# Chunk attention with a two-layer MLP: a list scheduler in the source, and both layers of the MLP by seven products

## The chip, the cores and the metric

One core of one Trainium2 chip. The time is device time in microseconds (us) of one launch. Three runs of the kernel before took 285.93, 286.01 and 288.08 us; their median, 286.01, is the time before. Lines written L171 are lines of the kernel before, unless the kernel after is named.

## The reference

```python
scores = scale * np.matmul(q_c, k_c.transpose(0, 1, 2, 4, 3))
scores = scores - np.max(scores, axis=-1, keepdims=True)
attn = np.exp(scores)
attn = attn / (np.sum(attn, axis=-1, keepdims=True) + 1e-09)
out = np.matmul(attn, v_c)
...
x = np.ascontiguousarray(attn_out.transpose(0, 2, 1, 3)).reshape(B * S, H * D)
...
h = x @ w_in
g = np.maximum(0.01 * h, h)
return (g @ w_out).astype(np.float32)
```

q, k and v are 8 batches x 8 heads x 576 tokens x 64; each chunk of 64 tokens attends only to itself, with scale 1/8. The result, put side by side over the heads, is x of 4608 tokens x 512. Then comes an MLP: w_in is 512 x 2048, w_out 2048 x 512, with a leaky ReLU between, here called the first and the second layer. The output is 4608 x 512 in fp32.

## The kernel before, in words

*Attention* goes by groups of 128 tokens (two chunks, all 8 heads): 36 groups, numbered u = 0 to 35. POOL issues the loads of q, k (L73) and v (L82), and of both weights (L89, L101), cast to fp16 on the way; only the first group's q and k come as fp32 through other queues. TensorE (PE) needs q and k turned. For the first nine groups (UD = 9) PE turns them (L542, L547) and VectorE (DVE) and ScalarE (ACT) copy them out; for the rest SP issues DMA transposes (stage_t, L567), and POOL copies q into the zero-padded tile QZ (L576). Then, for each group: scores on PE (L583); on DVE their maximum mx (L593) and its subtraction sh (L598); the exponential ex on ACT (L605); on DVE the row sum z (L612), the small constant ze (L614), the reciprocal zi (L616) and the normalization en (L622). en is turned by PE for the first nine groups (L631, with the copy et at L638), by a DMA transpose that SP issues for the others (L644). The values product xp = et x v follows on PE (L657), and ACT copies it into the ring xT of 1536 tokens (L673), the input of the first layer.

*The MLP* goes by blocks of tokens: six of 128, three of 256, six of 512 (BLOCKS). The first layer is always the plain product (mm1, L171): four 128-row steps for each 128 of the 2048 hidden units, 512 columns of PSUM to a unit of work; ACT applies the leaky ReLU while it copies PSUM to gT in fp16 (act1, L191). The second layer of the blocks of 128 and 256 is the plain product (mm2, L203). For the six blocks of 512 tokens it goes by seven products instead of eight (Strassen's way, L298): g is cut into 2 x 2 parts (256 tokens x 1024 hidden units), w_out into 2 x 2 parts (1024 x 256), and each product multiplies a part, or a sum of parts, of each. The sums of w_out (WF, L234) are made once. DVE makes the sums of gT for each block (form, L263), 128 x 2048 elements each. The products go into three PSUM tags, ma, mb and mc, two banks of work at a time; DVE and ACT combine them (combine, L334 to L343; evict, L352 to L356) into the output tile osb. The last block does this in halves (piece, L364 to L390), so that its stores go out in pieces.

*The order* is written in two ways. For the first groups it stands by hand in a string (FRONT, L724), with idle products between (L681). From group 5 on a loop over groups (L757 to L787) fixes where each group's attention stages go, and fill(n) puts units of MLP work on PE between them. pick() takes the first unit whose inputs are due by running sums of the time that PE, DVE and ACT have been given (T). Each of eight PSUM banks has a fixed purpose: a tag each for transposed q and k (shared with ma and mb), scores, values, and four for MLP units, of which mc takes one.

## Time and profile before

| | |
|---|---|
| Runs | 285.93, 286.01, 288.08 us |
| Span of the profiled execution | 285.7 us |
| Instructions | 7255 |
| Matmuls and transposes on PE | 3012 |
| Instructions on DVE, ACT, POOL (as counted in the profile) | 322, 264, 166 |
| Moved by DMA | 39.14 MB |

The profiled execution's span lies 0.3 us under the median of the runs. A page gives each engine's busy time, its share of the span and the number of its instructions; groups of instructions by source line, with busy time and the mean duration of one in ns; and the chain of waits, followed back from the last instruction. PEld is the weight load of PE, which runs beside its matmuls. A busy engine is not always one that works at its pace: matmuls are pipelined, and their durations in the trace overlap. Rows such as "52.70 0.89 PE hT L171 x16" of the chain are start, length, engine, tile, line and number of instructions.

### The profile page before, as it was taken

The numbers are of one execution on the slowest core, as the hardware profiler recorded it, in microseconds if no ns is written. First come the engines' busy times: TensorE is split into PE (matmuls) and PEld (weight loads), VectorE is DVE, ScalarE is ACT, GpSimd is POOL, SyncE is SP. The second block draws the span as 40 slices with busy tenths as digits, with TensorE's granted clock in tenths as the row PEclk, the third lists the DMA queues.
The fourth block names the chain that finished last, engine by engine and source line by source line (L and its number), as shares of the span: only waits on it lengthen the run. The fifth ranks groups of instructions, "written<-read, shape, count | busy, mean of one in ns | idle before, by whom it ended". The sixth has DMA issues, their size and how long they took to land.

```text
span 285.7 us, 7255 instructions
## 1 busy us (share of the span) xinstructions
PE 275.5 (96%) x3012; PEld 226.3 (79%) x3012; DVE 193.8 (68%) x322; ACT 149.4 (52%) x264; POOL 128.1 (45%) x166
## 2 busy tenths in 40 slices
PE   4979999999999999999999999999999999999995
PEld 4969855877949585899989899998999998666784
DVE  6987515666687776557888888888888840820392
ACT  6347733655738374777356546554565554535320
POOL 8846646876585647657538495332410000000000
PEclk9999999999999999999999999999999999999999
DMA  9999999999999999999999999999714301200213
GB/s 131 170 189 179 192 165 195 143 180 162 175 147 173 158 156 184 162 157 134 155 154 158 139 188 197 153 136 249 114 30 112 93 2 73 76 0 0 110 59 129
DMA packets 165825, 39.14 MB, mean 137 GB/s; under 512 B 156832, under 2 KB 161440, under 8 KB 165792
## 3 DMA queue, kind: packets, MB, share of 16 engines
q0 software_dynamic: 114336, 18.09, 91.5%
q1 hardware_dynamic: 50416, 20.33, 42.8%
q8 instruction: 23, 0.38, 0.5%
q10 hardware_dynamic: 1040, 0.26, 0.4%
q14 instruction: 10, 0.08, 0.1%
HBM read 36.70 MB, written 9.44 MB: 161 GB/s over the span
## 4 chain that ended last, share of the span: by engine, by line
PE 84%; DMA 6%; DVE 5%; ACT 2%; issue 1%; POOL 1%; ACTq 0%; POOLq 0%
PE hT L171 40%; PE oP L203 15%; PE mb L298 10%; PE mc L298 7%; PE ma L298 6%; DMA k_in<-in_k_dram 4%; PE xp L657 3%; PE Sp L583 2%; DMA VB<-in_v_dram 2%; DVE S L263 2%; ACT ex L605 1%; ACT gT L191 1%; DVE en L622 1%; PE kp L547 1%; DVE sh L598 0%
## 5 line engine op out<-in xcount | busy, mean ns | idle before, releaser
L171 PE MATMUL hT<-xT,w_inT 128*128 128x256 f16 (+2 forms) x1344 | 143.4, 257 | 1.9 <-DMA w_inT<-in_moe_w_in_dram 0.9
L171 PEld LDWEIGHTS <-w_inT 128*128 128x128 f16 x1344 | 107.6, 98 | 15.6 <-issue 2.6
L191 ACT ACTIVATE gT<-hT 128x512 f16<-128x512 f32 x144 | 85.5, 595 | 54.5 <-PE hT L171 53.3
L576 POOL COPY QZ<-QT 64x512 f16<-64x512 f16 x54 | 36.5, 676 | 53.0 <-DMA QT<-q_in 34.1
L203 PE MATMUL oP<-w_outT,gT 128*128 128x512 f16 x192 | 44.9, 379 | 0.0
L298 PEld LDWEIGHTS <-gT 128*128 128x128 f16 x384 | 37.5, 98 | 6.2
L605 ACT ACTIVATE ex<-sh 128x512 f16<-128x512 f32 x36 | 22.6, 627 | 33.7 <-DVE sh L598 33.6
L73 POOL DMA_DIRECT2D k_in<-in_k_dram x39 | 32.9, 845 | 15.9 <-DVE z L612 4.1
L612 DVE TENSOR_REDUCE z<-ex 128x8 f32<-128x512 f16 x36 | 24.7, 685 | 21.1 <-ACT ex L605 20.9
L593 DVE TENSOR_REDUCE mx<-Sp 128x8 f32<-128x512 f32 x36 | 24.7, 686 | 18.1 <-PE Sp L583 18.0
L73 POOL DMA_DIRECT2D q_in<-in_q_dram x39 | 33.2, 851 | 7.0 <-DMA w_outT<-in_moe_w_out_dram 2.4
L298 PEld LDWEIGHTS <-S 128*128 128x128 f16 x288 | 28.1, 98 | 5.0 <-DVE S L263 0.5
L203 PEld LDWEIGHTS <-gT 128*128 128x128 f16 x192 | 17.6, 98 | 17.7
L622 DVE TENSOR_TENSOR en<-ex,zi 128x512 f16<-128x512 f16 x36 | 27.2, 757 | 1.2
L673 ACT ACTIVATE xT<-xp 128x512 f16<-128x512 f32 x36 | 21.3, 592 | 9.4 <-PE xp L657 9.4
L598 DVE TENSOR_TENSOR sh<-Sp,mx 128x512 f32<-128x512 f32 x36 | 24.9, 691 | 1.2
L298 PE MATMUL mb<-WF,gT 128*128 128x256 f16 x192 | 24.6, 273 | 0.0
L263 DVE TENSOR_TENSOR S<-gT 128x2048 f16<-128x2048 f16 x18 | 22.3, 1278 | 1.5 <-ACT gT L191 1.5
L82 POOL DMA_DIRECT2D VB<-in_v_dram x16 | 18.5, 1161 | 0.0
L215 ACT ACTIVATE osb<-oP 128x512 f32<-128x512 f32 x12 | 7.2, 597 | 18.4 <-PE oP L203 18.4
L657 PEld LDWEIGHTS <-VB 128*128 128x128 f16 x288 | 13.1, 98 | 3.1 <-issue 0.6
L583 PEld LDWEIGHTS <-QZ 128*128 128x128 f16 x288 | 13.2, 99 | 2.2 <-issue 0.3
(57 smaller groups left out, 233.2 us busy)
## 6 DMA issues: line engine op xcount, KB each, us to landing
out_dram<-osb SPq DMA_DIRECT2D x10, 512.0 KB, 3.5
VB<-in_v_dram POOLq DMA_DIRECT2D x16, 288.0 KB, 13.2
q_in<-in_q_dram POOLq DMA_DIRECT2D x31, 128.0 KB, 13.1
k_in<-in_k_dram POOLq DMA_DIRECT2D x31, 128.0 KB, 13.6
out_dram<-osb SPq DMA_DIRECT2D x14, 256.0 KB, 6.8
w_inT<-in_moe_w_in_dram POOLq DMA_DIRECT2D x8, 256.0 KB, 9.7
w_outT<-in_moe_w_out_dram POOLq DMA_DIRECT2D x4, 512.0 KB, 9.9
q_in<-in_q_dram POOLq DMA_DIRECT2D x8, 64.0 KB, 9.1
```

The source lines that it names most:

```text
L73: nc.gpsimd.dma_start(out=t[a - r0:z - r0], in_=src[a // S, :, a % S:a % S + z - a, :].rearrange("h p d -> p h d"),)
L171: nc.tensor.matmul(out=hT[:, i, :], lhsT=w_inT[:, t, fc * 128:(fc + 1) * 128], rhs=xT[:, t, r0 % RING:r0 % RING + tb], start=(t == 0), sto ...
L191: nc.scalar.activation(out=gT[j][:, nf * a:nf * a + nf, h * tb:h * tb + tb], in_=HT.pop((j, a, h)), func=AFT.Prelu, bias=0.0, scale=1.0, a ...
L203: nc.tensor.matmul(out=o, lhsT=gT[j][:, fc, ti * 128:(ti + 1) * 128], rhs=w_outT[:, fc, :], start=(n == 0 and fc == part * 4), stop=(n == ...
L263: nc.vector.tensor_tensor(out=to, in0=of, in1=by, op=op)
L298: nc.tensor.matmul(out=BANK[bank][:, p, :] if j < LAST else ENDS[bank, p], lhsT=lhs[:, fc, p * 128:(p + 1) * 128], rhs=rhs[:, fc, :], star ...
L576: nc.gpsimd.tensor_copy(out=QZ[u % NQZ][part, :, :, s, :], in_=qt[part])
L593: nc.vector.tensor_reduce(out=MX[u], in_=SP[u], axis=AXL.X, op=ALU.max)
L598: nc.vector.tensor_tensor(out=SH[u], in0=SP.pop(u), in1=MX.pop(u).unsqueeze(2).to_broadcast((128, 8, CH)), op=ALU.subtract)
L605: nc.scalar.activation(out=E[u], in_=SH.pop(u), func=AFT.Exp, bias=0.0, scale=SCL)
L612: nc.vector.tensor_reduce(out=z, in_=E[u], axis=AXL.X, op=ALU.add)
L622: nc.vector.tensor_tensor(out=E[u], in0=ex, in1=ZI.pop(u).unsqueeze(2).to_broadcast((128, 8, CH)), op=ALU.mult)
```

## The change

The kernel is rewritten. What it computes is the same; these parts differ.

*The order is planned by a program in the source.* Every instruction, or short run of them, becomes a task with an engine (or several that may take it, each with a cost), a key (when it is wanted), the tasks on which it depends and the buffers that it takes. Buffers are rings with as many places as RINGS says; eight PSUM banks form one ring that all uses share. Plan.run walks through time: on each engine it takes, of the tasks that can start first, the one with the lowest key. A task that several engines may take goes to the one where it ends first with what is queued there; so q's copies into QZ, the copies of PSUM, ze and en may go to DVE, ACT or POOL. The keys come from the places of the MLP's units on PE and from a table of numbers, NUDGE.

*The blocks* are four of 128 tokens (0 to 3) and eight of 512 (4 to 11). PE turns the first eight groups instead of nine. q and k have 7 places instead of 9.

*The first layer* of blocks 5 to 11 goes by seven products instead of eight, that of block 4 by the plain product in pieces of 256 tokens, that of blocks 0 to 3 plain. x is cut into 2 x 2 parts (256 of the 512 inputs x 256 tokens), w_in into 2 x 2 parts (256 x 1024). DVE makes four sums of x for each block (xs) and, once, four of w_in (FI). Each block has four chains; in each, three PSUM banks X, Y and V hold two 128-row pieces of hidden units. P5 opens V and is copied to p5; P1 opens X, and X is copied to Y, PSUM to PSUM; P6 is added in X; DVE sets V = X + p5; P7 is added in X; DVE sets w = X + p5; P4 is added in X; P2 is added in Y and P3 in V. Four leaky evictions (c11 from Y, c12 from V, c22 from w, c21 from X) write gT.

*The second layer* of blocks 4 to 11 goes by seven products in another form, whose products also are added in three PSUM banks X, Y and V, in the order P1, P2, P6, P5, P7, P4, P3. It has three sums of w_out (FO), and a fourth that overwrites a part of w_outT. DVE makes the sums S1 to S4 of gT, each in two instructions of 128 x 1024 elements. X is copied to p1, u2 and u3 between its products, and DVE adds them to Y or V into osb. The last block goes in two chains of one 128-token piece each.

The core of the diff:

```diff
+        def behind(t, e, at):
+
+            return self.lean.get(e, 0.0) + max(now[e], at) + t.engs[e] + sum(x.engs[e] for x in ready[e] if x.key < t.key and x.eng == e)
...
+                    ahead = min(loads, key=lambda c: c[1].key)
+                    can = [c for c in can if c not in loads or c is ahead]
+                first = min(c[0] for c in can)
+                c = min((c for c in can if c[0] <= first + slack), key=lambda c: c[1].key)
+                if best is None or c[0] < best[0]:
...
+KNOBS = {'LEAD': 9.24,
+ 'PACE': 3.62,
+ 'UD': 8,
+ 'L1_PLAIN': (0,),
+ 'LEAN': {'DVE': -0.13, 'POOL': -0.48, 'ACT': -0.13},
+ 'LOADS': 'Q0 g3 g7 v0 g1 Q1 g4 Q3 P1 Q2 P0 g6 P2 P3 v1 g5 g2',
+ 'NUDGE': {'s': -3.18,
+           'Q4': -14.46,
+           'zv.0.0': 51.85,
...
+    PLAIN = 4
+    NB = (NU - PLAIN) // 4
...
-    BLOCKS = [128] * 6 + [256] * 3 + [512] * 6
-    PLAIN = 9
...
+    LEAD, PACE, LEAN, NUDGE, LOADS = (KNOBS[n] for n in ("LEAD", "PACE", "LEAN", "NUDGE", "LOADS"))
+    UD, L1_PLAIN = KNOBS["UD"], KNOBS["L1_PLAIN"]
...
+    RINGS = {
+        "bank": 8, "qk": 7, "QT": 4, "KT": 5, "QZ": 3, "mx": 2, "sh": 2, "ex": 2, "z": 2, "en": 4, "et": 4,
+        "xs": 2, "p5": 2, "w": 2, "gT": 2, "S1": 1, "S2": 1, "p1": 1, "u2": 1, "u3": 1, "osb": 3,
+    }
...
+    def need(u):
+        j = block_of(u)
+        back = 0 if j < PLAIN else 3 - (u - PLAIN) % 4
+        return at1[j] - back * PACE - LEAD + NUDGE.get(f"need{u}", 0.0)
...
+
+        ts = task(f"s.{u}", PE, 0.24, key + 0.5, emit_s, deps=ready, bufs=[qz, kt], opens=[sp], bank="full")
+        tm = task(f"m.{u}", DVE, 0.6, key + 0.6, emit_m, deps=[ts], bufs=[sp], opens=[mx])
+        tb = task(f"b.{u}", DVE, 0.6, key + 0.61, emit_b, deps=[tm], bufs=[sp, mx], opens=[sh])
+        tx = task(f"x.{u}", ACT, 0.52, key + 0.7, emit_x, deps=[tb], bufs=[sh], opens=[ex])
+        tz = task(f"z.{u}", DVE, 0.71, key + 0.8, emit_z, deps=[tx], bufs=[ex], opens=[z])
+        tz = task(f"ze.{u}", {DVE: 0.2, POOL: 0.3}, 0, key + 0.801, emit_ze, deps=[tz], bufs=[z])
+        tz = task(f"zi.{u}", DVE, 0.24, key + 0.802, emit_zi, deps=[tz], bufs=[z])
+        tn = task(f"n.{u}", {DVE: 0.61, POOL: 1.0}, 0, key + 0.81, emit_n, deps=[tz], bufs=[ex, z], opens=[en])
...
+            td = task(f"d.{u}", SP, 1.3, key - 15.0, emit_d, deps=[tn], bufs=[en], opens=[et], after=("turn", 0.0, 1))
...
+    fi = sums("fi", DVE, 1.14, (
+        (lambda: FI[:, 0], ADD, lambda: A21, lambda: A22, ()),
+        (lambda: FI[:, 1], SUB, lambda: FI[:, 0], lambda: A11, (0,)),
+        (lambda: FI[:, 2], SUB, lambda: A11, lambda: A21, ()),
+        (lambda: FI[:, 3], SUB, lambda: A12, lambda: FI[:, 1], (1,)),
+    ), [key_fi + i for i in range(4)], [t for x in wi.values() for t in x])
...
+    def forms_out(plain):
+        return sums("fo", DVE, 1.14, (
+            (lambda: FO[:, 0], SUB, lambda: B12, lambda: B11, ()),
+            (lambda: FO[:, 1], SUB, lambda: B22, lambda: FO[:, 0], (0,)),
+            (lambda: FO[:, 2], SUB, lambda: B21, lambda: FO[:, 1], (1,)),
+            (lambda: B12, SUB, lambda: B22, lambda: B12, (0,)),
+        ), [key_fo + i for i in range(4)], [t for x in wo.values() for t in x] + rows[0] + cv, tail=plain)
...
+        ts = sums("xs", DVE, 0.34, (
+            (lambda: mem(xs)[:, 0], SUB, lambda: x12, lambda: x11, ()),
+            (lambda: mem(xs)[:, 1], SUB, lambda: x22, lambda: mem(xs)[:, 0], (0,)),
+            (lambda: mem(xs)[:, 2], SUB, lambda: x22, lambda: x12, ()),
+            (lambda: mem(xs)[:, 3], SUB, lambda: x21, lambda: mem(xs)[:, 1], (1,)),
+        ), [k0 - 2, k0 - 1, k0, k0 + 1], us, opens=[xs], of=f".{j}")
...
+            P5 = product("P5", "V", FI[:, 0], 0, XS(0), True, 0, [fi[0], ts[0]], [xs], bufs=bufs)
+            P1 = product("P1", "X", w_inT[:, 0:2], 0, lambda: x11, True, 1, us + W, bufs=bufs)
...
+            c5 = task(f"p5.{j}.{n}", MOVE, 0, key + 1.0 * UNIT, move(lambda p5=p5: mem(p5), lambda ps=ps: ps["V"]), deps=[P5], bufs=[bV], opens=[p5])
+            cy = task(f"y.{j}.{n}", MOVE, 0, key + 1.1 * UNIT, move(to_y, lambda ps=ps: ps["X"]), deps=[P1], bufs=[bX], opens=[bY], bank="seed")
+            P6 = product("P6", "X", FI[:, 1], 0, XS(1), False, 2, [cy, fi[1], ts[1]], [xs], bufs=bufs)
+            P2 = product("P2", "Y", w_inT[:, 2:4], 0, lambda: x21, False, 3, [cy] + us + W, bufs=bufs)
+
+            def emit_z(ps=ps, p5=p5):
+                nc.vector.tensor_tensor(out=ps["V"], in0=ps["X"], in1=mem(p5), op=ADD)
+
+            def emit_w(ps=ps, p5=p5, w=w):
+                nc.vector.tensor_tensor(out=mem(w), in0=ps["X"], in1=mem(p5), op=ADD)
+
+            tz = task(f"z.{j}.{n}", DVE, 0.6, key + 2.5 * UNIT, emit_z, deps=[P6, c5], bufs=[bX, bV, p5])
+            P7 = product("P7", "X", FI[:, 2], 0, XS(2), False, 4, [tz, fi[2], ts[2]], [xs], bufs=bufs)
+            P3 = product("P3", "V", FI[:, 3], 0, lambda: x22, False, 5, [tz, fi[3]] + us, bufs=bufs)
+            tw = task(f"w.{j}.{n}", DVE, 0.6, key + 4.5 * UNIT, emit_w, deps=[P7, tz], bufs=[bX, p5], opens=[w])
+            P4 = product("P4", "X", w_inT[:, 2:4], HF, XS(3), False, 6, [tw, ts[3]], [xs], bufs=bufs)
+            readers[j] += [P1, P2, P3]
...
+            evict("Y", 0, 0, 4, [P2], [bY], "c11")
+            evict("V", 0, 1, 6, [P3], [bV], "c12")
+            evict("w", HB, 1, 6.5, [tw], [w], "c22")
+            evict("X", HB, 0, 7, [P4], [bX], "c21")
...
+            ORDER = ("P1", "P2", "P6", "P5", "P7", "P4", "P3")
+            into = {"P1": "X", "P6": "X", "P7": "X", "P4": "X", "P2": "Y", "P5": "V", "P3": "V"}
+            bufs = {"X": bX, "Y": bY, "V": bV}
+            key = {m: k0 + span * i / 7 + shift for i, m in enumerate(ORDER)}
...
-    ORDER = (3, 2, 1, 5, 4, 6, 7)
...
+    for j in range(NJ):
+        if j == PLAIN:
...
+        if j < PLAIN:
+            done = layer1_plain(j, 128)
+            plain += layer2_plain(j, done)
+        else:
+            done = layer1_plain(j, 256) if j - PLAIN in L1_PLAIN else layer1_seven(j)
+            layer2_seven(j, done)
...
-    ROUND = [0] * 6 + [6] * 33
-    for it in range(6, NU + 3):
...
-        if it <= NU:
...
-        due = free_v[:]
-        values(it - 2 if it - 2 < UD else it - 3 if it - 3 >= UD else -1)
-        fill(ROUND[it] - 4)
-        for b in due:
...
+    for emit in plan.run(filler=(filler, emit_idle)):
+        emit()
```

At the start, POOL issues the loads in another order. The kernel before, from v's first batch on (q_in and k_in are a group's rows, VB v's, w_inT x4 two quarters of w_in):

```order
L82 DMA VB_63<-in_v_dram 64x36x64 x2
L73 DMA q_in<-in_q_dram 128x8x64
L73 DMA k_in<-in_k_dram 128x8x64
L89 DMA w_inT<-in_moe_w_in_dram 64x4x512 x4
L73 DMA q_in<-in_q_dram 128x8x64
L73 DMA k_in<-in_k_dram 128x8x64
L89 DMA w_inT<-in_moe_w_in_dram 64x4x512 x4
L73 DMA q_in<-in_q_dram 64x8x64 x2
```

The kernel after, from v's first batch on, behind the first quarter of w_in and groups 3 and 7 (qk is q or k of one group):

```order
L396 DMA VB_114<-in_v_dram 64x36x64 x2
L390 DMA qk_66<-in_q_dram 128x8x64
L390 DMA qk_66<-in_k_dram 128x8x64
L402 DMA w_inT<-in_moe_w_in_dram 64x4x512 x2
L390 DMA qk_67<-in_q_dram 64x8x64 x2
L390 DMA qk_67<-in_k_dram 64x8x64 x2
L402 DMA w_inT<-in_moe_w_in_dram 64x4x512 x2
L408 DMA w_outT<-in_moe_w_out_dram 128x4x512
```

w_in comes in quarters between the groups' loads instead of in two halves, the first quarter ahead of everything, and w_out (w_outT) in single quarters between them.

In the second half of the program, DVE before (two attention groups and, between, the combination of the second layer's products and one sum of gT):

```order
L616 RECIPROCAL zi<-ze 128x8
L622 TENSOR_TENSOR en<-ex,zi 128x512
L336 TENSOR_TENSOR tw<-mc,td 128x512
L263 TENSOR_TENSOR gT<-gT 128x8x256
L593 TENSOR_REDUCE mx<-Sp 128x8
L598 TENSOR_TENSOR sh<-Sp,mx 128x512
L612 TENSOR_REDUCE z<-ex 128x8
L614 TENSOR_SCALAR ze<-z 128x8
L616 RECIPROCAL zi<-ze 128x8
L622 TENSOR_TENSOR en<-ex,zi 128x512
L338 TENSOR_TENSOR tt<-tw,osb 128x512
```

DVE after, in the stage of blocks 5 to 11 (S is a sum for the second layer; bank at L836 is V = X + p5, w at L839 is X + p5, p the copied P5, u and osb the second layer's):

```order
L1003 TENSOR_TENSOR S_107<-gT_104,S_107 128x1024 x2
L836 TENSOR_TENSOR bank<-bank,p_100 128x512
L647 RECIPROCAL z_89<-z_89 128x8
L641 TENSOR_REDUCE z_88<-ex_86 128x8
L836 TENSOR_TENSOR bank<-bank,p_101 128x512
L979 TENSOR_TENSOR osb_111<-bank,p_108 128x2x256
L839 TENSOR_TENSOR w_102<-bank,p_100 128x512
L647 RECIPROCAL z_88<-z_88 128x8
L839 TENSOR_TENSOR w_103<-bank,p_101 128x512
L479 COPY p_100<-bank 128x512
L631 TENSOR_REDUCE mx_82<-bank 128x8
L634 TENSOR_TENSOR sh_84<-bank,mx_82 128x512
```

The additions and copies of the first layer's chains stand between the steps of the softmax, which are now further apart; two of its steps, ze and en, are not on DVE there.

They are on POOL. POOL before, in the same stage, copies q into QZ and issues loads:

```order
L576 COPY QZ_67<-QT 64x8x64 x2
L82 DMA VB_63<-in_v_dram 64x36x64 x2
L73 DMA q_in<-in_q_dram 128x8x64
L73 DMA k_in<-in_k_dram 128x8x64
L576 COPY QZ_65<-QT 64x8x64 x2
L73 DMA q_in<-in_q_dram 128x8x64
L73 DMA k_in<-in_k_dram 128x8x64
```

POOL after (L644 is ze, L650 is en, L390 the loads):

```order
L479 COPY QZ_81<-QT_73 64x8x64
L479 COPY QZ_80<-QT_71 64x8x64 x2
L644 TENSOR_SCALAR z_89<-z_89 128x8
L390 DMA qk_69<-in_q_dram 128x8x64
L650 TENSOR_TENSOR en_90<-ex_87,z_89 128x512
L644 TENSOR_SCALAR z_88<-z_88 128x8
L390 DMA qk_69<-in_k_dram 128x8x64
L650 TENSOR_TENSOR en_91<-ex_86,z_88 128x512
```

ze and en of 25 and 20 of the 36 groups stand in POOL's queue, among the copies and the issuing of loads. In all, DVE has 412 rows' instructions instead of 322, ACT 338 instead of 265, POOL 183 instead of 166.

1381 lines of the change are left out of this document (769 added, 612 removed), and 6 rows, old and new, of the table FRONT.

## The prediction

> **What bounds the kernel now.** I read the page's busy lines first, then busy time by stretches, then the chain of waits, then the groups by shape.
>
> ```profile
> span 285.7 us, 7255 instructions
> PE 275.5 (96%) x3012; PEld 226.3 (79%) x3012; DVE 193.8 (68%) x322; ACT 149.4 (52%) x264; POOL 128.1 (45%) x166
> PEclk9999999999999999999999999999999999999999
> ```
> ```profile
> 0.00:24.00 24.00, 18.14 (x284) 16.70 (x284) 18.68 (x38) 11.86 (x19) 16.83 (x27) 1.00 1.56 167
> 24.00:130.00 106.00, 105.15 (x1202) 79.32 (x1199) 66.97 (x120) 61.34 (x108) 69.33 (x86) 1.00 1.87 168
> 130.00:234.00 104.00, 103.82 (x1152) 93.54 (x1151) 88.11 (x138) 57.81 (x106) 41.90 (x54) 1.00 1.37 136
> 234.00:270.00 36.00, 36.00 (x276) 26.15 (x274) 10.60 (x12) 15.55 (x27) 0.00 (x0) 1.00 0.12 45
> ```
> The columns are stretch, length, then PE, PEld, DVE, ACT, POOL busy, granted clock, DMA share and GB/s. From 24 us on PE is idle for little more than 1 us in 246; VectorE is next, 88.11 of 104 us. TensorE is the bound, at full clock, so the change is priced by PE time taken out, less what PE must newly wait for. A busy PE need not run at its pace, so I take the pace from the chain of waits, where pieces follow without a gap:
>
> ```profile
> 49.65 0.23 PE xp L657 x8
> 51.84 0.86 PE oP L203 x4
> 52.70 0.89 PE hT L171 x16
> 53.60 0.22 PE tpe L631 x4
> 147.86 0.87 PE mb L298 x8
> 280.79 1.76 PE mb L298 x16
> ```
> That is 0.029 us for 64 columns, 0.0556 for 128, 0.109 for 256, 0.216 for 512. The counts:
>
> ```profile
> L171 PE MATMUL hT<-xT,w_inT 128*128 128x256 f16 x768 | 95.8, 273 | 0.2 <-ACT xT L673 0.2
> L203 PE MATMUL oP<-w_outT,gT 128*128 128x512 f16 x192 | 44.9, 379 | 0.0
> L171 PE MATMUL hT<-xT,w_inT 128*128 128x128 f16 x512 | 31.7, 219 | 1.8 <-DMA w_inT<-in_moe_w_in_dram 0.9 <-issue 0.7
> L298 PE MATMUL mb<-WF,gT 128*128 128x256 f16 x192 | 24.6, 273 | 0.0
> L171 PE MATMUL hT<-xT,w_inT 128*128 128x512 f16 x64 | 16.3, 379 | 0.0
> ```
> First layer: 768 x 0.109 + 512 x 0.0556 + 64 x 0.216 = 126.0 us. Second: 192 x 0.216 = 41.5, and six blocks by products, 6 x 7 x 2 x 8 = 672 x 0.109 = 73.2. Together 240.7. Attention adds 36 x 0.46 for scores and values and 27 x 0.22 for transposes: 22.5. So 263.2 of the 285.7 us is necessary PE work; the last product ends at 282.5, a tail of 3.2, and 19.3 is lost, nearly all before 37 us.
>
> **The change, part by part.** *Products.* After, the first layer has 4 x 64 = 256 matmuls of 128 columns, one plain block of 128 of 256, and seven blocks x 28 products x 4 = 784 of 256: 256 x 0.0556 + 912 x 0.109 = 113.6. The second has 64 x 0.216 and 8 x 112 = 896 x 0.109: 111.5. Together 225.1, so 15.6 us go. Eight instead of nine groups turned by PE saves 12 transposes, 0.7. With loss and tail as they are: 285.7 - 16.3 = **269.4**.
>
> *Start.* The first big block needs groups 4 to 7. With both weights, v of two batches and the first group in fp32 that is 4.2 + 7 x 0.26 + 1.15 + 0.77 = 7.9 MB as written. The rate of 0 to 24 us above gives 4.0 MB, and the rest comes at the rate of this row:
>
> ```profile
> 24.00:50.00 26.00, 25.20 (x314) 18.76 (x311) 12.48 (x27) 13.46 (x25) 16.26 (x20) 1.00 1.83 181
> ```
> So 24 + 3.9 / 0.181 = 46 us, with some 28 us of four plain blocks to do until then: 18 us lost, as now. The next eight groups are wanted about 5 us each sooner, with their transposes issued by SP. Bounds 0 (loads run ahead, as now) and 5 (nothing covers it); I take 1.0, near the lower end since the loss computed equals today's.
>
> *Values.* Each group's scores pass DVE, ACT, DVE, POOL or DVE, and a DMA transpose. Before, PE has 15 us of other work in between (first two rows, group 12); after, the order puts 10.9 to 12.0 us of matmuls there for four of the last-needed groups (10.9 for two), over 13.4 elsewhere.
>
> ```profile
> 87.49 0.40 PE L583 MATMUL Sp<-KT,QZ 128*128 128x64 f16 x8
> 102.65 0.40 PE L657 MATMUL xp<-et,VB 128*128 128x64 f16 x8
> ```
> ```profile
> 176.03 0.68 DVE L593 TENSOR_REDUCE mx<-Sp 128x8 f32<-128x512 f32 x1
> 176.75 0.69 DVE L598 TENSOR_TENSOR sh<-Sp,mx 128x512 f32<-128x512 f32 x1
> 178.19 0.69 DVE L612 TENSOR_REDUCE z<-ex 128x8 f32<-128x512 f16 x1 [0.76 <-ACT ex L605]
> 179.36 0.69 DVE L622 TENSOR_TENSOR en<-ex,zi 128x512 f16<-128x512 f16 x1
> 179.97 0.68 DVE L338 TENSOR_TENSOR tt<-tw,osb 128x512 f32<-128x512 f32 x1
> ```
> ```profile
> et<-en SPq DMA_TRANSPOSE x6, 7.5
> ...
> et<-en SPq DMA_TRANSPOSE x4, 2.4
> ```
> From mx to the end of en is 4.0 us; the transpose lands in 7.5 us while loads run (140 to 170 us) and 2.4 when they have stopped (after 210). So 11.5 to 12, plus queueing behind other DVE work, about 1.5. Against the four covers that is 2.7 + 2.7 + 2.0 + 1.6 = 9 us late at most, nothing at 2.4. I take 2.5: loads end about then, and DVE and ACT catch up while PE waits. POOL takes 20 of the 36 normalizations (en), which no row shows on POOL: at least its copy of half the elements, at most twice the DVE row's slowest instance:
>
> ```profile
> 154.75 1.28 POOL L576 COPY QZ<-QT 64x512 f16<-64x512 f16 x2 [0.86 <-PE xp L657]
> 161.48 2.16 POOL L576 COPY QZ<-QT 64x512 f16<-64x512 f16 x2 [3.73 <-DMA QT<-q_in]
> 161.63 1.53 DVE L263 TENSOR_TENSOR S<-gT 128x2048 f16<-128x2048 f16 x1
> 174.90 1.22 DVE L263 TENSOR_TENSOR gT<-gT 128x2048 f16<-128x2048 f16 x1
> ```
> 0.6 to 1.8 us; I take 1.1, inside the 1.5 above. [...]
>
> *Round trips.* Each group of a first layer by products goes P1, copy to a second bank, P6, add, P7, add, P4 (numbers of the code): three trips from PE through ACT or DVE and back, 84 in all. In the order mostly three foreign products stand in each gap, 3 x 0.436 = 1.31 us. A trip needs one such operation, 0.60 on ACT (L191: 595 ns) or 0.68 on DVE, and under 0.1 of hand-over: 0.7 if the engine is free, 1.3 behind one other. DVE decides how often it is free. Between the first sums of blocks 5 and 11 PE has 168 x 0.436 + 75 x 0.872 + 44 x 0.23 = 148.8 us of work. DVE has 240 instructions there: 151 of the 512-element kind above, which follow each other at 0.61 us (179.97 less 179.36), 42 of 1024 fp16 elements at 0.60 (half of 1.13, the start to start of the gT row, up to 1.13), 24 of 512 at 0.33 and 23 short ones at 0.2: 130 us, and some 7 for results that the next one needs: 92%. In the stage from 130 us it is 85% by durations, and (88.1 - 138 x 0.09) / 104 = 73% counted so, since neighbours overlap by 0.09. It is not the bound, but seldom free. Bounds for the trips: 0, and 84 x 0.25 = 21 us. I take 2.5, near the lower end, since 92% still leaves 11 us to catch up.
>
> The row of 161.63 lasts 0.3 longer than that of 174.90, and POOL's copies beside it 0.9 longer in all. [...]
>
> *Rest.* ScalarE has 338 instructions instead of 265 in the order, 73 x 0.6 = 44 us on its 149, 70% of the time. The two folded weight sets cost DVE 8 x 1.2 us (five before) while PE has plain blocks. Stores are as many bytes. The tail ends with a 256 KB store instead of 128 KB: 0 to 1.8 us more, I take 0.6. Sum: 269.4 + 1.0 + 2.5 + 2.5 + 0.6 = **276.0**; the runs' median stands 0.3 above the profiled span, within this.
>
> **Rivals.** *Full cover:* order and buffers hide all trips and values: 269.4 to 271.5. For it: PE idles 1 us in 246 today. Against it: three trips where there was none, and short covers. *Late values:* the 9 us come whole: 269.4 + 1 + 9 + 2.5 + 0.6 = 282.5. For it: 7.5 us of landing until 190 us; against it, only four covers are short. *VectorE bounds:* its waits for ACT's exponentials stay as they are,
>
> ```profile
> ACT ex L605 <- DVE sh L598: 33.6, 21, 2.7
> DVE z L612 <- ACT ex L605: 20.9, 29, 1.5
> ```
> which is 0.6 us a group (20.9 / 36), 13 for 22 groups. [...] For it: 92%; against it, the order puts other DVE work into those gaps. *Slower:* the engine in a round trip is behind two operations instead of one half the time, so that a trip takes 0.25 to 0.3 longer than its cover: 84 x 0.27 = 23, giving 269.4 + 23 + 1.6 = 294. It decides from 0.23 us a trip on (19.5 / 84). For it: engines are in order and DVE is 92% full. Against it: P2, P3 and second-layer products can absorb part.
>
> **How the numbers follow.** My forecast, 271.5 to 281, has 0.60; full cover 0.12; late values 0.08; VectorE as the bound 0.07; slower 0.13. I predict 276.0. The range 269 to 285 takes in both middle rivals and leaves out the slow one. One per cent, about what a measurement here can tell, is 283.1 and 288.9. Faster has 0.60 + 0.12 + 0.07 (half of the middle ones, which straddle 283.1) = 0.79, same 0.08, slower 0.13.
>
> **What would show it.** Right: 912 and 896 matmuls of 256 columns at 0.87 for eight; PE idle by 4 to 8 us after 40 us, in pieces under 1 us before FI and w_inT products (waiting for DVE or ACT) and 1 to 3 us before a values product of blocks 9 to 11 (waiting for DMA et); DVE near 240 to 250 us busy. Wrong: PE idle over 2 us in each block waiting for DVE, en on POOL over 2 us with DVE's reciprocal waiting for POOL, or a first second-layer product later than 42 us.

## The result, and the profile after

The changed kernel takes 306.4 us (median of four runs, 304.7 to 306.8) against 285.97 before: a ratio of 1.069, interval 1.0645 to 1.0735. The forecast of 276.0 us is 30 us off, on the wrong side, and outside its range. Where single runs of an experiment lay over 1.5% above its fastest (one run of the control with half loads took 1021.6 us, unexplained), the times below are medians of the others. The profiled execution took 304.71 us with a span of 302.9, so 17.2 us more span than before.

The busy lines of the page for the kernel after:

```profile
span 302.9 us, 7399 instructions
PE 267.9 (88%) x2925; PEld 232.5 (77%) x2925; DVE 228.5 (75%) x412; ACT 184.9 (61%) x335; POOL 139.7 (46%) x183
PEclk9799999999778899995999999999999999999999
```

PE is busy for less time than before (275.5), but in a longer span, and four stretches ran at half clock (0.50 granted): 11.5 to 15, 80 to 87, 97 to 100 and 138 to 145 us. Where the time went stands in the stages. Kernel before, then after; columns as in the prediction: stretch, length, PE, PEld, DVE, ACT, POOL busy, granted clock, DMA share and GB/s:

```profile
0.00:60.00 60.00, 53.30 (x728) 43.14 (x729) 37.53 (x75) 30.88 (x52) 41.37 (x55) 1.00 1.78 169
60.00:180.00 120.00, 119.82 (x1316) 97.84 (x1314) 91.35 (x151) 70.96 (x126) 76.22 (x97) 1.00 1.85 164
180.00:280.00 100.00, 99.80 (x951) 83.27 (x950) 63.30 (x95) 47.60 (x87) 10.47 (x14) 1.00 0.55 85
```
```profile
0.00:60.00 60.00, 49.05 (x648) 40.96 (x649) 45.77 (x86) 30.88 (x55) 40.05 (x54) 0.97 1.82 177
60.00:180.00 120.00, 100.92 (x1067) 86.28 (x1063) 86.21 (x154) 78.30 (x142) 74.03 (x92) 0.93 1.83 154
180.00:280.00 100.00, 98.98 (x1052) 88.94 (x1050) 85.05 (x151) 69.91 (x128) 25.66 (x37) 1.00 0.58 86
```

Busy time hides slow and filling products, so I count each stage's matmuls in the trace, without those on the tile idle, at the paces of the prediction (0.029 us for 64 columns, 0.0556, 0.109 and 0.216 for 128, 256 and 512). What the stage is longer than that is lost:

| stage, us | work before | lost before | work after | lost after |
|---|---|---|---|---|
| 0 to 60 | 42.4 | 17.6 | 36.9 | 23.1 |
| 60 to 180 | 119.4 | 0.6 | 93.6 | 26.4 |
| 180 to 280 | 99.4 | 0.6 | 98.3 | 1.7 |
| 280 to the span's end | 2.3 | 3.4 | 18.3 | 4.6 |
| sum | 263.5 | 22.2 | 247.1 | 55.8 |

The work fell by 16.4 us, as forecast, and the loss rose by 33.6: 5.5 before 60 us, 25.8 in the middle stage, 2.3 after. That is the 17.2 of the span. Of the 25.8, 18.9 are idle time more than before. Of the other 6.9, an estimated 5.6 are work at half clock: in the three such stretches of this stage PE worked for some 11 us behind its waits. From 180 us on, with the same chains of products, PE loses 1.7 us in 100.

What PE waits for, kernel after (engine and line waited for: us in total, times, longest):

```profile
PE bank L685 <- DMA et<-en: 10.9, 3, 5.4
PE bank L557 <- ACT qk L477: 7.5, 2, 5.4
PE bank L625 <- POOL QZ L479: 7.1, 2, 6.1
```

L685 is the values product of an attention group, L625 its scores, and L557 the transposes of the first group at the start (5.4 us of that wait is the time before the first data, which the kernel before has too: its first transpose runs at 5.12). The longest of the scores' waits and of the values' waits, from PE's timeline:

```profile
83.54 0.61 PE L625 MATMUL bank<-KT,QZ 128*128 128x64 f16 x8 [6.07 <-POOL QZ L479]
...
97.33 0.61 PE L685 MATMUL bank<-et,VB 128*128 128x64 f16 x8 [5.40 <-DMA et<-en]
```

By the order the first is group 12's scores, which wait for the copy of its q by POOL, the second group 11's values. Follow them back on the queues that feed them. POOL:

```profile
69.80 0.88 POOL L390 DMA_DIRECT2D qk<-in_k_dram  x1 [1.00 <-DMA qk<-in_k_dram]
70.67 0.86 POOL L479 COPY QZ<-QT 64x512 f16<-64x512 f16 x1
71.62 0.23 POOL L644 TENSOR_SCALAR z<-z 128x8 f32<-128x8 f32 x1
75.21 0.94 POOL L390 DMA_DIRECT2D qk<-in_q_dram  x1 [3.36 <-DMA VB<-in_v_dram]
78.42 0.88 POOL L390 DMA_DIRECT2D qk<-in_k_dram  x1 [2.26 <-DMA VB<-in_v_dram]
79.31 1.06 POOL L650 TENSOR_TENSOR en<-ex,z 128x512 f16<-128x512 f16 x1
80.67 0.94 POOL L390 DMA_DIRECT2D qk<-in_q_dram  x1 [0.30 <-DMA qk<-in_q_dram]
81.60 0.88 POOL L390 DMA_DIRECT2D qk<-in_k_dram  x1
82.53 0.95 POOL L479 COPY QZ<-QT 64x512 f16<-64x512 f16 x1
```

The copy that releases group 12 is the last row; its input, the transposed q, had landed at 74.83. It stands behind four loads of groups 16 and 19, of which the two of group 16 were issued only when older loads had landed (3.36 and 2.26 us). Group 8's normalization (79.31) stands behind the same two, though its reciprocal had been ready since 72.1, and that is how group 11 came late: its exponential on ACT waited 6.02 us for group 8's normalization, since the tile ex has only two places.

```profile
80.40 0.63 ACT L638 ACTIVATE ex<-sh 128x512 f16<-128x512 f32 x1 [6.02 <-POOL en L650]
```
Group 11's own normalization follows on POOL at 85.25. SP, in the same stretch:

```profile
73.32 0.56 SPq L888 DMA_DIRECT2D out_dram<-osb  x1
80.43 1.19 SPq L578 DMA_TRANSPOSE QT<-qk  x1
81.73 1.21 SPq L578 DMA_TRANSPOSE KT<-qk  x1
83.03 1.33 SPq L675 DMA_TRANSPOSE et<-en  x1
84.46 1.28 SPq L578 DMA_TRANSPOSE KT<-qk  x1
85.85 1.46 SPq L578 DMA_TRANSPOSE QT<-qk  x1
87.40 3.90 SPq L675 DMA_TRANSPOSE et<-en  x2
```

SP issues nothing for 6.5 us: the transpose of group 15's q waits for its load, which landed at 80.38. The transpose of group 14's k stands behind it, though its load had landed at 69.24. The transposes of the normalized scores of groups 8, 10 and 11 stand there too, but these scores were ready only at 80.4, 83.0 and 86.3. Group 11's is the second of 87.40; issued by 91.3, landing some 6 us later. Both queues hold back ready work because a load in front of it is late. How late is shown by the time from issue to landing of four loads issued from 41 to 46 us and of four issued from 63 to 66, the last of them group 17's k. The first line answers for the early ones, the second for the late ones (both by tile; the second takes in three DMA transposes too, and its four loads alone took 17.0 to 17.4 us):

```profile
DMA to landing us min/median/max: 7.7/7.9/8.3
```
```profile
DMA to landing us min/median/max: 7.2/17.0/17.4
```

By issue and landing times about eight loads are under way in both stretches, and the landing takes twice as long. Two halves of v are ahead of the late four, which by the fit given with the experiments are worth 4.5 us against 1.6 for as many loads of q or k. What else comes in between, from 50 us on, is SP's DMA transposes and a store.

The kernel before has this lateness too. POOL's waits there, and the landings around its q loads issued from 60 to 80 us (the four loads took 12.3 to 16.4 us; the shorter times are of three DMA transposes):

```profile
POOL QZ L576 <- DMA QT<-q_in: 34.1, 15, 6.2
```
```profile
DMA to landing us min/median/max: 7.6/12.3/16.4
```

There it costs PE nothing: group 12's scores run at 87.49 and its values at 102.65 (rows in the prediction), 15 us apart. After, PE had come to group 12's scores at 77.47 (83.54 less 6.07), 10 us sooner, since one block of 512 takes four groups at once.

The start, ACT after, and before:

```profile
6.04 0.59 ACT L477 ACTIVATE QZ<-bank 64x512 f16<-64x512 f16 x1 [0.70 <-PE bank L557]
9.42 0.63 ACT L492 ACTIVATE xs<-p 64x512 f16<-64x512 f32 x1 [2.79 <-DMA p<-in_v_dram]
10.06 0.59 ACT L477 ACTIVATE QZ<-bank 64x512 f16<-64x512 f16 x1
10.55 0.40 ACT L477 ACTIVATE qk<-u 128x256 f16<-128x256 f32 x1
```
```profile
5.32 0.42 ACT L704 ACTIVATE k_in<-k_f 128x256 f16<-128x256 f32 x1 [0.45 <-DMA k_f<-in_k_dram]
```

After, half of the first k is converted at 10.55, behind a conversion of v that waited 2.79 us for its load; before, at 5.32. The first scores follow at 11.92 instead of 7.53, the first values at 19.98 instead of 13.17.

### The profile page after: what moved, and what is told of

Its sections match the earlier page's. It is cut to its first block, busy times and chain, and to the rows that moved or that the text cites. A ratio compares the mean times of both kernels' runs of the same rounds, so it can differ in the third digit from the quotient of the medians.

```text
span 302.9 us, 7399 instructions
## 1 busy us (share of the span) xinstructions
PE 267.9 (88%) x2925; PEld 232.5 (77%) x2925; DVE 228.5 (75%) x412; ACT 184.9 (61%) x335; POOL 139.7 (46%) x183
## 4 chain that ended last, share of the span: by engine, by line
PE 67%; DMA 11%; DVE 8%; issue 5%; POOL 4%; ACT 3%; SPq 1%; POOLq 0%; ACTq 0%
PE bank L962 28%; PE bank L812 25%; DMA et<-en 8%; PE bank L765 5%; PE bank L876 3%; PE bank L685 3%; POOL qk L390 3%; DMA p<-in_v_dram 2%; DVE S L908 2%; PE bank L625 2%; DVE mx L631 1%; DVE sh L634 1%; POOL QZ L479 1%; ACT QZ L477 1%; DVE xs L712 1%
## 5 line engine op out<-in xcount | busy, mean ns | idle before, releaser
L743 ACT ACTIVATE gT<-bank 128x512 f16<-128x512 f32 x116 | 67.1, 596 | 32.2 <-PE bank L812 21.3
L962 PEld LDWEIGHTS <-gT 128*128 128x128 f16 x512 | 50.6, 101 | 7.8 <-issue 1.1
L812 PE MATMUL bank<-xs,FI 128*128 128x256 f16 x336 | 49.5, 274 | 1.2 <-DVE xs L712 0.7
L962 PE MATMUL bank<-w_outT,gT 128*128 128x256 f16 x384 | 50.0, 280 | 0.2
L812 PEld LDWEIGHTS <-FI 128*128 128x128 f16 x448 | 43.2, 99 | 7.2 <-issue 1.6
L962 PEld LDWEIGHTS <-S 128*128 128x128 f16 x384 | 36.9, 98 | 5.0 <-DVE S L908 0.8
L390 POOL DMA_DIRECT2D qk<-in_k_dram x39 | 33.3, 854 | 15.7 <-DMA VB<-in_v_dram 5.5
L390 POOL DMA_DIRECT2D qk<-in_q_dram x39 | 33.9, 870 | 13.7 <-DMA VB<-in_v_dram 5.7
L812 PEld LDWEIGHTS <-w_inT 128*128 128x128 f16 x336 | 32.7, 98 | 3.9
L962 PE MATMUL bank<-FO,S 128*128 128x256 f16 x256 | 32.9, 273 | 0.3 <-DVE S L908 0.3
L812 PE MATMUL bank<-xT,w_inT 128*128 128x256 f16 x224 | 32.6, 273 | 0.0
L765 PE MATMUL bank<-xT,w_inT 128*128 128x128 f16 (+1 forms) x384 | 30.4, 237 | 1.5 <-DVE QZ L479 0.7
L765 PEld LDWEIGHTS <-w_inT 128*128 128x128 f16 x384 | 27.0, 98 | 3.6 <-issue 1.3
L839 DVE TENSOR_TENSOR w<-bank,p 128x512 f32<-128x512 f32 x28 | 19.1, 682 | 11.3 <-PE bank L812 11.1
L479 POOL COPY QZ<-QT 64x512 f16<-64x512 f16 x26 | 18.7, 720 | 18.8 <-PE bank L625 12.2
L650 POOL TENSOR_TENSOR en<-ex,z 128x512 f16<-128x512 f16 x20 | 21.2, 1062 | 10.0 <-issue 5.4
L396 POOL DMA_DIRECT2D VB<-in_v_dram x16 | 18.6, 1166 | 15.3 <-PE bank L685 10.1
L836 DVE TENSOR_TENSOR bank<-bank,p 128x512 f32<-128x512 f32 x28 | 19.4, 694 | 6.7 <-PE bank L812 5.6
```

Source lines behind the costliest of these rows:

```text
L390: nc.gpsimd.dma_start(out=to[a - r0:z - r0, which], in_=src[a // S, :, a % S:a % S + z - a, :].rearrange("h p d -> p h d"),)
L479: (nc.vector if eng == DVE else nc.gpsimd).tensor_copy(out=to(), in_=of())
L650: (nc.gpsimd if eng == POOL else nc.vector).tensor_tensor(out=mem(en), in0=mem(ex), in1=mem(z)[:, 2].unsqueeze(2).to_broadcast((128, 8, CH ...
L743: nc.scalar.activation(out=to, in_=of, func=AFT.Prelu, bias=0.0, scale=1.0, alpha=0.01)
L765: nc.tensor.matmul(out=t["h"][:, i, :], lhsT=w_inT[:, n, fc * 128:(fc + 1) * 128], rhs=xT[:, n, r0 % RING:r0 % RING + tb], start=(i == 0 a ...
L812: nc.tensor.matmul(out=ps[to][:, i, :], lhsT=lhs[:, t, f:f + 128], rhs=rhs()[:, t], start=(opens and i == 0 and t == 0), stop=(t == 1), sk ...
```

## The experiments

The theory before the first run: attention groups reach PE late because loads are late and the in-order queues of POOL and SP hold ready work behind them (*supply*). Rivals: POOL alone, with its new normalizations (*queue*); the round trips of the first layer's products (*trips*); the low clock (*clock*). Beside the experiments the kernel before ran on the same chip, at medians of 286.2 to 286.8 us; ratios and their intervals, as on record, are against that, and can differ by a few thousandths from a quotient of the medians. Without a word on it, an experiment changes the kernel after.

**POOL emptied.** Everything that the order gives POOL, except its loads and fillings, is issued on ACT or DVE, at the same place in the order.

```diff
+OFF_POOL = {"p0": ACT, "p1": ACT, "ze": DVE, "n": DVE}
-            order.append((start, lambda t=t: t.emit(t.eng) if ...
+            order.append((start, lambda t=t: t.emit(OFF_POOL.get(t.name.split(".")[0], POOL) if t.eng == POOL else t.eng) if ...
```

> The plan and the order are those of the kernel after, but what it gave to POOL other than loads is issued elsewhere: the copies of q into QZ by ACT, ze and en by DVE. Supply theory (PE waits because the QZ copies and the normalizations stand in POOL's queue behind load issues, which themselves wait for earlier loads to land): the idle of 6.1 us before the scores at 83.5 us and most of the 5.4 us before the values at 97.3 go, with the low clock behind them; 306.4 - 8 to 12 = 294 to 298. Round-trip theory (the first layer's chains lose the time on a VectorE that is nearly full): VectorE gets 20 x 0.6 + 25 x 0.1 = 15 us more, so no gain or a loss, 306 to 318.

310.1 us, ratio 1.0797 (1.0745 to 1.0848): no faster, and not the 294 to 298 of the supply theory but inside the range given for the trips. PE's waits:

```profile
PE bank L687 <- DMA et<-en: 10.6, 4, 4.8
PE bank L559 <- ACT qk L479: 8.2, 2, 5.4
PE bank L627 <- DMA KT<-qk: 6.4, 2, 5.8
```

With POOL out of the path, group 12's scores do come sooner, at 78.34 instead of 83.54. But now group 14's wait as long (at 90.77) for the transpose of their k, which SP issues at 83.34, again behind the one that waits for group 15's q. POOL's queue is one place where the lateness shows; with it emptied, SP's is the next.

**Half of the loads.** From group 8 on only four of eight heads of q and k are loaded (the others keep old data); order, transposes and products are untouched.

```diff
-                    out=to[a - r0:z - r0, which],
+                    out=to[a - r0:z - r0, which, :H if u < 8 else H // 2],
```

> Order as in the kernel after; from group 8 on each load of q and k brings only four of the eight heads (half of the bytes and packets; the other four heads keep what the place held before), all else is computed as it was. Supply theory, its rate part (loads land too late because loads and transposes share the DMA engines): the q and k loads from 40 to 170 us cost half, the waits of POOL for earlier loads fall from some 25 us to under 10, and the PE idle at 77 to 98 us shrinks by over half; 286 to 295. If only the place in POOL's queue counts and not the rate: 300 to 306. Round-trip theory: 304 to 308.

287.1 us, 1.0017 (0.9986 to 1.0047): 19.3 us come back.

```profile
60.00:180.00 120.00, 113.81 (x1272) 99.73 (x1271) 103.94 (x185) 93.03 (x169) 77.63 (x103) 1.00 1.60 147
```

PE gains 12.9 us in the stage, and the clock is full. The control is the same cut in the kernel before, from group 9 on:

> The kernel before, with q and k loads of half of the heads from group 9 on (the other heads keep what the place held). Control for the run with half loads. If the kernel before is bound by TensorE and its loads are hidden: 284 to 287. If it is itself held up by loads, so that half loads make any kernel faster: 276 or less.

285.4 us, 0.9956 (0.9935 to 0.9977). Before, the lateness of loads costs 1.2 us; after, about 19.

**Half of the DMA transposes.** From the sixth such group on, q and k are transposed for half of the heads only; all loads stay.

```diff
+                out=mem(rings[which])[:, :4 if u in FULL else 2].rearrange("p i e t -> p i (e t)"),
+                in_=mem(QK[u])[:, which, :H if u in FULL else H // 2].rearrange("p h d -> p (h d)"),
```

> The kernel after, order unchanged; the DMA transposes of q and k turn half of the heads from the sixth such group on (groups 8 to 11 and 13 whole; elsewhere the other half of the turned tiles keeps what it held). Loads are whole. If each DMA transpose takes about 0.8 us of the engines that carry the loads, some 46 halved ones give back up to 18 us of DMA time, half of it before 110 us: 290 to 300. If transposes do not hold back loads, only their own landing is shorter: 302 to 307.

294.7 us, 1.0299 (1.0275 to 1.0323): 11.7 us come back though not a byte less is loaded. By the traces, POOL's loads of q and k issued from 80 to 160 us land in a median of 6.1 us instead of 10.7, and the transposes of q and k in 6.4 instead of 7.7. The transposes hold back the loads.

**PE turns twelve groups instead of eight** (`'UD': 12`), so that the order has 12 fewer DMA transposes early on (of q, k and normalized scores).

> One number: PE turns twelve groups instead of eight, so that the first block by seven products (groups 8 to 11) needs no DMA transpose; the planner orders everything anew. 12 DMA transposes go, at about 1.1 us each of DMA time beside loads, and 4 x 0.66 = 2.6 us of PE work come. Supply theory: the loss between 60 and 100 us (15.8 us) falls by 8 to 14 and the total is 295 to 301. Round-trip theory: 306.4 + 2.6 = 309 or more.

305.1 us, 1.0618 (1.0544 to 1.0691), in neither range. The stage from 60 us gains 7.7 us of busy PE, part of it the added transposes, and from 180 us 3.6 are lost: the shortage moved.

**The first layer plain in all eight blocks** (`'L1_PLAIN': (0, 1, ..., 7)`): no round trips there, 7 x 1.74 = 12.2 us more of products.

> The first layer of all eight blocks of 512 tokens goes by the plain product in pieces of 256 tokens; the planner orders everything anew. PE work rises by 7 x 16 x 0.109 = 12.2 us; the 84 round trips go, and 28 x 6 instructions of 512 elements on ACT and DVE less 28 x 4 evictions that stay. Round-trip theory: the loss of some 30 us against the sum of products mostly goes, 285 to 298. Supply theory: PE waits for groups 8 to 15 as before, some 5 us of the added work lie in that wait, 308 to 316.

332.2 us, 1.1568 (1.1511 to 1.1625), above both ranges. That is 25.8 us worse, twice the added products; PE's waits for et rise from 10.9 to 18.6 us. If trips were the cause, taking them out should have given time back. The same with the better prices of the next part but one:

> The planner's prices as in the run with prices alone, and the first layer plain in all blocks of 512. If the first layer by products pays its 12.2 us of PE work in full once loads are in time: 12 us above the run with prices alone, 289 to 296 (the plan ends at 289). If the round trips eat the gain: within 5 us of it.

308.8 us, the middle of two runs (306.8 and 310.8), too few for an interval: 13.6 more than with those prices alone (295.2). By the count of matmuls its work is 12.3 us more. So with better prices the plain layer costs about what its products cost, as the first of the two forecasts says of the difference, and the round trips eat next to nothing of the gain. Trips fall as a cause. Why the plain layer cost 13 us beyond its products in the order with the old prices is open; 7.7 us of it are the longer waits for et.

**The clock held.** 60 idle products of 128 columns ahead of each of three long waits.

```diff
+WARM = ('s.12', 'v.11', 'v.17')
...
+            if name in WARM:
+                emit_idle(60, buf.slot)()
```

> The kernel after, with 60 idle products of 128 columns (3.3 us) on PE right ahead of the three instructions at which it idled over 4 us: the scores at 83.5 us (group 12) and the values at 97.3 and 139.6 (groups 11 and 17). In after the clock was granted at half for 6.8, 3.4 and 6.8 us behind these waits. If the low clock is what makes a wait cost more than itself, it stays at 1 there and 5 to 8 us come back: 298 to 302. If the supply of groups is late by the same amount whatever PE does in between, the time returned by the clock only lengthens the next wait: 304 to 308.

305.4 us, 1.068 (1.0652 to 1.0709): the same time, with a mean clock of 0.989 instead of 0.964. PE around two of the waits:

```profile
78.08 3.51 PE L1055 MATMUL idle<-ident 128*128 128x128 f16 x60
...
83.73 0.61 PE L632 MATMUL bank<-KT,QZ 128*128 128x64 f16 x8 [2.14 <-POOL QZ L481]
...
98.05 0.41 PE L693 MATMUL bank<-et,VB 128*128 128x64 f16 x8 [2.58 <-DMA et<-en]
```

Group 12's scores run at 83.73 (83.54 without) and group 11's values at 98.05 (97.33). Work done faster in between only waits longer: the supply sets these times, and the low clock is what follows from the waits.

**Right prices for the planner.** In the source, a DMA transpose costs the loads nothing and a load lands 1.4 us after its turn. From the loads in four traces (before, after and two experiments) I fitted the time between landings: 0.80 us for q or k of a group, 2.25 for half a batch of v, 0.81 more for each DMA transpose issued in between, 0.98 for each store. These are estimates. Put into the planner, with the loads of the weights priced higher as well, which then makes another order:

```diff
+        busy = self.load_free > end
...
-            land = self.load_free + 1.4
+            land = self.load_free + 3.0
...
-            self.turn_free = max(self.turn_free, start + t.us) + 0.6
-            land = self.turn_free + (7.0 if self.load_free > start + t.us else 2.0)
+            self.load_free += 0.82 * busy
+            land = end + (6.3 if busy else 2.2)
...
+            self.load_free += 1.0 * (busy and kind == "store")
```

> Only the planner's prices of DMAs are changed, to those that the landings in the traces of before, after and the first experiments give: a DMA transpose holds back the loads behind it by 0.82 us (after: by nothing), a store by 1.0 (nothing), a load lands 3.0 us behind its turn (1.4), half a batch of v takes 2.25 us (2.0). All tasks, keys and the table stay; the order on every engine is planned anew. Supply theory (loads and DMA transposes share the DMA engines, the plan did not know, so POOL and SP have loads and transposes in an order in which what PE needs stands behind what lands late): the loss from 60 to 180 us (25 us) mostly goes; the plan ends at 277, so 277 to 284. If the DMA engines are simply too slow for this kernel in any order: 297 to 306. Round-trip theory: 303 to 308.

295.2 us, 1.0281 (1.0230 to 1.0332): 11.2 us come back from the order alone, with the kernel's work unchanged. That lies between the supply theory's 277 to 284 and the 297 to 306 of engines too slow in any order. With half loads as well:

> The planner's prices as in the run with prices alone, and q and k loads of half of the heads from group 8 on (the others keep what the place held). Supply theory: what the run with prices alone still loses between 90 and 170 us (16 us) was again late loads, and goes: 276 to 283, which leaves the products, the start (6 us worse than before) and the end. If something else in the new order holds PE (round trips, VectorE, banks): 288 to 295.

287.6 us, 1.0040 (1.0017 to 1.0063), where 276 to 283 was expected of the supply theory; it lies just under the other range. The stages:

```profile
0.00:60.00 60.00, 47.37 (x613) 39.63 (x614) 44.93 (x81) 27.48 (x48) 38.03 (x54) 1.00 1.66 169
60.00:180.00 120.00, 115.04 (x1283) 100.95 (x1281) 108.93 (x193) 90.75 (x165) 75.74 (x103) 1.00 1.56 147
180.00:280.00 100.00, 99.17 (x1023) 88.70 (x1021) 82.09 (x146) 59.68 (x111) 18.56 (x28) 1.00 0.36 77
```

Hardly any wait for a DMA is left, and still 18.4 us are idle, 12.6 of them before 60 us (6.7 in the kernel before) and 5.0 in the middle, in waits under 2 us for ACT and DVE. Supply explains about 19 of the 30 us by which the forecast missed; the start is the next largest part. The first v's loads, which the planner has at 4.0 us, priced at 8.0:

> The run with prices, and one price more: the four loads of the first batch of v through SP's and ACT's queues land 8.0 us after issue (the plan had 4.0; the trace of after shows 6.4 to 7.5, that of the run with prices 8 to 9 on ACT). In after the copy of that v stands in ACT's queue ahead of half of k's cast and waits 2.79 us for it, so that the first group's scores come at 11.9 us (before: 7.5). If the start is lost there: first scores at 9 us or earlier, 3 to 5 us less idle before 60 us, and 290 to 293 in all. If the supply from 90 us on sets the time whatever the start does: 294 to 297.

294.4 us, 1.0239 (1.0182 to 1.0296), 0.8 us better than with the first prices, inside the intervals. The first scores came at 10.09 us, not at 9 or earlier, and a gain at the start is not seen in the time.

**Better plans.** The planner's tables were searched anew, off the chip, with prices near the fitted ones (1.05 for a DMA transpose, 1.4 for a store), and with en turned by PE in 16 instead of eight groups in the best plan. Three plans ran:

> All measured prices (transposes 1.05, loads 0.82 and 2.3, stores 1.4, first v 8.0) and the table of keys, the lead and the number of groups turned by PE (10, and en of 12) moved by hill climbing on the plan's own end with these prices and with worse ones. Supply theory with a mistaken plan: 278 to 288, below before. If the order can't make up for shared DMA engines: 290 to 297.

> As the run before, from another start of the climb: 8 groups of q and k and 16 of en turned by PE, so 20 + 28 x 2 DMA transposes instead of 84. 278 to 288 by the theory of a mistaken plan, 290 to 297 otherwise.

> As the two before, third start: 9 groups of q and k and 12 of en turned by PE, keys of the groups 5.7 us earlier. 278 to 288 by the theory of a mistaken plan, 290 to 297 otherwise.

291.95 us, 1.0160 (1.0102 to 1.0218); 286.24, 0.9986 (0.9950 to 1.0023); 288.8, 1.0084 (1.0046 to 1.0121). The second's middle stage:

```profile
60.00:180.00 120.00, 114.45 (x1295) 101.31 (x1293) 103.36 (x193) 95.11 (x175) 77.37 (x94) 1.00 1.98 161
```

All 20 us that the changed kernel lost come back by another order and by en of eight more groups turned by PE, with full loads and the same products by sevens. What each of the two gives is not separated. And three plans made with prices worse than measured, for slack:

> The plan made with prices worse than the measured ones (a DMA transpose holds loads back by 1.2 us and lands 7.2 us behind its issue while loads run, a load of q or k 0.86, half a batch of v 2.5, 2.9 us behind its turn), so that what PE needs next is there even when DMAs are late; the first loads of k and v with the prices of the trace; keys climbed again (9 groups of q and k and 13 of en turned by PE). If the run with the tuned keys still loses by waits for late DMAs and the start: 279 to 284, faster than both kernels. If a better order has no more to give: 285 to 289.

> The same prices, another climb: 9 groups of q and k and 19 of en turned by PE. 280 to 285 if late DMAs and the start are what is left, 285 to 290 otherwise.

> The same prices, a third climb: 10 groups of q and k and 16 of en turned by PE. 280 to 285 if late DMAs and the start are what is left, 285 to 290 otherwise.

290.4 us, 1.0139 (1.0094 to 1.0183); 291.3, 1.0161 (1.0128 to 1.0193); 289.5, 1.0106 (1.0067 to 1.0144). All three miss the range given for late DMAs and the start, and the first two lie above the other range as well: these prices gave no better order. The first has a full middle stage and a poor start:

```profile
0.00:60.00 60.00, 45.24 (x603) 37.33 (x604) 42.11 (x73) 29.41 (x53) 38.31 (x52) 1.00 1.83 173
60.00:180.00 120.00, 115.70 (x1289) 101.34 (x1287) 104.25 (x195) 91.59 (x169) 69.35 (x86) 1.00 1.77 149
```

Its plan had put a load of v ahead of the first k's on ACT's queue, so that k's conversion waited until 10.96 us. Whether a start in time would be kept or given back, the last run asks: the same plan with k's load ahead of v's.

> The plan of e13_safe_a, made again with k's first load ahead of v's on ACT's queue and its landing priced at 3.8 us instead of 2.3 and the first v's at 7.5. In e13_safe_a k's conversion waited until 10.96 us and PE was busy for 45.24 of the first 60 us, with 115.70 of 120 in the stage from 60 us. If what is left above the kernel before is the late start, the first scores come near 8 to 9 us and PE is busy for 48 to 50 us of the first 60, with the middle stage as full as there (115 or more): the time is 291.3 less 3 to 5, so 286 to 288. If a gain at the start is given back in the middle, as in e11_prices_v, the first stage gains and the middle falls below 114, and the time is 289 or more. Below 283.4 (faster by over 1%) I give a chance of 1 in 20.

287.0 us, 0.9984 (0.9954 to 1.0014): 3.4 us better, inside the range for a late start alone.

```profile
0.00:60.00 60.00, 49.91 (x650) 41.97 (x650) 43.82 (x79) 33.09 (x59) 38.27 (x52) 0.97 1.81 178
60.00:180.00 120.00, 116.52 (x1298) 101.83 (x1296) 106.05 (x195) 92.51 (x171) 70.75 (x90) 1.00 1.75 149
180.00:280.00 100.00, 99.36 (x1020) 88.34 (x1018) 80.64 (x145) 64.31 (x121) 20.57 (x27) 1.00 0.65 98
```

The start gains 4.7 us of busy PE, 2.9 by the count without products on idle, and the middle keeps its own. The first scores came at 10.46 us (13.31 without), not at 8 to 9. Counted like the table above, this plan has 248.8 us of work, 14.7 less than the kernel before, and 36.7 lost, 14.5 more: 6.4 more before 60 us, 5.8 in the middle, 1.3 to 280 and 1.0 behind. So it is level. No plan beat the kernel before.

## Why the prediction was wrong, point by point

*Products (15.6 and 0.7 us): right.* The groups after, L812 first layer and L962 second:

```profile
L812 PE MATMUL bank<-xs,FI 128*128 128x256 f16 x336 | 49.5, 274 | 1.2 <-DVE xs L712 0.7
L962 PE MATMUL bank<-w_outT,gT 128*128 128x256 f16 x384 | 50.0, 280 | 0.2
```

With the other operands they come to the forecast 912 and 896, and the work counted in the traces fell by 16.4.

*Start (1.0, at most 5): mis-sized, and by another mechanism.* It measured 5.5. Its time for the loads was right: the last of groups 1 to 7, the k of group 2, landed at 47.2 us (46 worked out), and the first second-layer product ran at 35.5, before the 42 that it set as a bound. By the count, 2.0 of the 5.5 us went before 20 us, 2.1 from 20 to 30 and 1.2 from 50 to 60. The prediction never followed the first group, whose k stands behind v's conversion on ACT's queue and whose values come 6.8 us later than before. That place in the queue is only a part: in the last run k goes first, and the first scores still come at 10.46 (7.53 before). The rest of the late start is not explained.

The same step had a sentence on the next eight groups, wanted about 5 us sooner each. It bounded them from 0, "loads run ahead, as now", to 5. Group 12 is one of them, wanted 10 us sooner, and the loads did not run ahead; PE's 7.1 us of waits for scores belong here.

*Values (2.5, at most 9): the step that failed.* Its parts were right: the transpose lands in 7.2 to 8.3 us from 80 to 110 us (7.5 forecast), and en on POOL takes 1.06 (1.1):

```profile
L650 POOL TENSOR_TENSOR en<-ex,z 128x512 f16<-128x512 f16 x20 | 21.2, 1062 | 10.0 <-issue 5.4
```

But it priced a chain from a group's scores on, as if the scores and each link's place in its queue were on time, and looked only at the cover behind them. It did not ask when a group's q and k land, nor what stands behind an issue that waits, though the step on the start noted that groups are wanted sooner and that SP issues their transposes. The trace of before had the warning, 34.1 us of POOL waiting for QT and loads that took 12.3 to 16.4 us. The prediction even shows one such wait (3.73 us, at 161.48), but reads only the copy's duration there. In the trace PE's waits for et alone are 10.9 us, over the bound of 9. In the runs late groups, by this step and by the sentence on the next eight, are most of the 25.8 us lost in the middle stage: half loads give back 19.3, half transposes 11.7, better prices 11.2, a better plan 20.2 (306.4 less 286.2). These are each by itself against the kernel after, and do not add up.

*Round trips (2.5) and the slower rival: not the cause.* The waits of L812 for DVE after come to 1.4 us at most, and from 180 us on, where all supply is there, PE idles 1.0 us in 100. The time came out slower than any rival, but not by the slower rival's mechanism: both plain first layers were slower still, the second by about its products.

*VectorE as the bound: no.* DVE is busy for 228.5 us, 75%, below the forecast 240 to 250. ACT's 184.9 us stand against 193 worked out.

*Late values (282.5): nearest in mechanism to what happened,* and still far short, since it let only the four short covers be late, by the landing of one transpose.

*Tail (0.6):* the last product ends at 299.5, 3.4 us before the span's end, 0.2 more than before.

The expected gain, then, is there in the work, and is lost from 60 to 180 us to late groups and before 60 us to the start. The last run mends most of the middle but not the start, which loses 24.0 us there against 23.1 in the kernel after. 14.5 us of loss over the kernel before are left against 14.7 of gain: 6.4 at the start, where the first scores and values come at 10.46 and 17.09 instead of 7.53 and 13.17, and 5.8 in the middle, of which 3.5 is idle, in small waits. Which single one of these waits could go is not tried.

## What to carry to other kernels

When a change lets the main engine reach a piece of work sooner, read in the trace of before when that work's inputs land and what waits for them today, on every queue; a wait that costs nothing under 15 us of cover is the next stall when the cover goes. In a queue that issues in order, ask of each instruction that may wait for a DMA what ready work stands behind it. And a planner that priced each queue's transfers alone made an order that the DMAs here did not keep (306.4 us, 295.2 with prices fitted to landings): fit its prices from landings in a trace first.

## What the runs showed of the hardware

A DMA transpose on SP's queue holds the loads of POOL's queue back by an estimated 0.81 us (the fit over loads of four traces), a store by 0.98. The half-transposes run shows the price: 11.7 us in all (294.7 against 306.4), with loads landing in a median of 6.1 us instead of 10.7.

In the trace of the kernel after the clock was granted at 0.50 in four stretches while PE still had work to come: for 3.4 us from 11.5, 6.8 from 79.8, 3.4 from 96.9 and 6.8 from 137.8 us. Each begins in a wait of PE or just behind one (2.10, 6.07, 5.40 and 4.22 us). With products in three of these waits the mean clock was 0.989 instead of 0.964 and the time 305.4 us instead of 306.4, with intervals of the ratios that overlap: here a low clock behind a late input cost little, since the next input was late too.

POOL's tensor_tensor of 512 fp16 elements a partition takes 1062 ns (20 of en in the kernel after), VectorE's of the same shape 686 (the other 16): 1.55 times. The factor of two in the prediction's upper bound for it was the author's estimate; no run shows it.
